# One group of scores per head pair from the third batch on, in an attention kernel followed by a feed-forward layer

## The chip, the cores and the metric

The kernel runs on one core of one Trainium2 chip. The time is device microseconds of one execution; what counts is the median of several. The engines are named as in the profile: PE (TensorE, matmuls), PEld (its weight loads), ACT (ScalarE), DVE (VectorE), POOL (GpSimd), SP (SyncE, which here only issues DMAs).

## The reference

Attention with a forget gate for 8 batches and 8 heads, 576 tokens, head width 64, and then a feed-forward layer over all 4608 tokens with 512 model columns and 2048 hidden ones:

```python
scores = scale * np.matmul(q, k.transpose(0, 1, 3, 2))
cum = np.cumsum(np.log(np.clip(f, 0.0001, 1.0)), axis=-1)
scores = np.where(causal, -1000000000.0, scores + cum[:, :, :, None] - cum[:, :, None, :])
attn = np.exp(scores - max) ; attn = attn / (sum + 1e-09)
x = np.matmul(attn, v)            # then heads side by side: 4608 x 512
h = x @ w_in
out = (h * (1.0 / (1.0 + np.exp(-h)))) @ w_out
```

## The kernel before

The decay factors are taken into the values: exp(-cum) of each key is multiplied into v, with one column of it kept as the 65th, so that a matmul of exponentials and values gives the outputs and the sums that they are divided by.

The first 128 queries of all heads are done in a prologue. The rest, 448 queries a head, is done in a loop over m = 0 to 15 (line 874, called a turn here), with two head pairs n = 2m and n + 1 in each; a batch has four head pairs, so m = 4 begins the third batch. For each head pair:

- `scores(n, c)`, lines 444 to 484: the scores, transposed, come in three chunks c = 0, 1, 2, each into one tile `sc` of two PSUM banks, one bank for each of the two heads. The two heads lie in partitions 0 to 63 and 64 to 127, so their matmuls (line 459) use half of the array's rows each. Then exponentials on ACT: 1024 wide for chunks 0 and 1 (line 463), 256 and 640 wide for chunk 2 (lines 463, 475). DVE masks with triangles (lines 468, 482).
- `attend(n)`, line 490: 28 matmuls of the exponentials with the values into one bank `dn` (lines 506, 515), then reciprocal and product on DVE into `xr` (lines 523, 524).
- `prepare(n)`, line 839: issues loads, casts on POOL and transposes by DMA for head pairs ahead. `back(m)`, line 531: turns the outputs of a turn, for m = 4 to 14 by DMA on SP, otherwise on PE.

The feed-forward layer is cut into pieces that are put between the attention's groups. An M1 piece (`m1_chunk`, line 560) is four matmuls into one bank `hp` (line 567), a tanh on ACT (line 575) and one product on DVE that reads both (line 576), after which the bank is free. An M2 piece (`m2_part`, line 594) is four matmuls 512 wide (line 612); four pieces fill one bank `po`, and the last of the four is followed by a copy `osb` on ACT (line 622), stored later from POOL's queue.

Which piece comes next is a planner's choice. `wanted` (line 641) keeps the M1 pieces of one group of tokens and the M2 pieces of the group before in step; `fill(us, least, ends)` (line 698) counts pieces at a fixed price (4 x (width / 2.4 + 2.5) ns) until `us` is used up, carries over what it went too far, and with `ends[0]` puts an M2 piece first. `slot(us, *ends)` calls it. `behind()` is the price of all pieces that are ready and not yet placed, and the last slot of a turn is the longer the more there is.

All engines work in the order in which the program states their instructions. PSUM's eight banks are two pools: `psc`, two buffers of two banks (tag "sc"), and `pbig`, four buffers of one bank (tag "big") for `hp`, `po`, `dn` and `tx`.

The loop's body before, whose lines matter for the change:

```python
scores(n, 0); scores(n, 1); prepare(n); back(m - 1); slot(2.4, 1, 0)
scores(n, 2); scores(n + 1, 0); prepare(n + 1);      slot(2.4, 1, 0)
scores(n + 1, 1); scores(n + 1, 2);                  slot(2.4, 1, 0)
attend(n); attend(n + 1);                            slot(0.8 to 3.5)
```

Of the kernel before, what the change touches and what calls it, by code (L numbers as in the profile page):

```python
# [8 lines left out]
ACT = mybir.ActivationFunctionType  # L9
ALU = mybir.AluOpType  # L10
FP32 = mybir.dt.float32
BF16 = mybir.dt.bfloat16
P = 128
# [5 lines left out]
def kernel(  # L19
# [10 lines left out]
    nc = tc.nc  # L30
# [410 lines left out]
    AT |= {(c, 0): SM + (c - 1) * P for c in range(1, NM)}  # L441
    AT |= {(2, 1): RB, (3, 1): SM + RB, (3, 2): 2 * SM}

    def scores(n, c):
        b, p = divmod(n, NP)
        if c == 0:
            us[n] = upool.tile([P, 2, UW], BF16, name="u", tag="u")
        u, ut = us[n], uts[n % 4]
        t = qkT[n]
        sc = psc.tile([P, 2, SM], FP32, name="sc", tag="sc")  # L450
        for kb, q0, q1, o in CHUNKS[c]:
            for i in range(2):
                r = slice(i * D, (i + 1) * D)
                if kb == 0:
                    kt = kT0[b][r, p, :]
                else:
                    k0 = RB if kb == NM else kb * P + RB
                    kt = t[r, k0 : k0 + P]
                nc.tensor.matmul(  # L459
                    sc[:, i, o : o + q1 - q0], lhsT=kt, rhs=t[r, q0:q1], start=True, stop=True  # L460
                )
        w = SM if c < 2 else T0
        nc.scalar.activation(  # L463
            out=u[:, :, c * SM : c * SM + w], in_=sc[:, :, 0:w], func=ACT.Exp, scale=scale
        )
        if c == 0:
            x = u[:, :, 0:RB].rearrange("p i (a t) -> p i a t", t=P)
            nc.vector.tensor_tensor(  # L468
                out=x,
                in0=x,  # L470
                in1=tri[:, None, None, :].to_broadcast([P, 2, NR, P]),
                op=ALU.mult,
            )
        if c == 2:
            nc.scalar.activation(  # L475
                out=ut[:, :, 0:3:2, :].rearrange("p k i t -> p i k t"),
                in_=sc[:, :, T0 : T0 + (NM + 1) * ST].rearrange("p i (k t) -> p i k t", t=ST),
                func=ACT.Exp,
                scale=scale,
            )  # L480
            x = ut[:, NM, 0:3:2, :]
            nc.vector.tensor_tensor(  # L482
                out=x, in0=x, in1=trit[:, None, :].to_broadcast([P, 2, ST]), op=ALU.mult
            )

    NGR = 2 * NR + 1

    BY_DMA = [2 * 2 <= m < NQ - 1 for m in range(NQ)]

    def attend(n):  # L490
        b, p = divmod(n, NP)
        if p % 2 == 0:
            xqs[n // 2] = xqp.tile([P, NGR, 2, D], BF16, name="xr", tag="xr", bufs=3)
        xq = xqs[n // 2]
        u, ut = us.pop(n), uts[n % 4]
        dn = pbig.tile([P, NGR, D + 1], FP32, name="dn", tag="big")

        def vals(kb, i):
            h = head(p, i)
            return v0[b][:, h, :] if kb == 0 else vbf[b][:, kb - 1, h, :]  # L500

        for i in range(2):
            for c in range(1, NM):
                for kb in range(c + 1):
                    o = AT[c, kb]
                    nc.tensor.matmul(  # L506
                        dn[:, i * NR + c - 1, :],
                        lhsT=u[:, i, o : o + P],
                        rhs=vals(kb, i),
                        start=(kb == 0),  # L510
                        stop=(kb == c),
                    )
        for i in range(2):
            for kb in range(NM + 1):
                nc.tensor.matmul(  # L515
                    dn[:, NGR - 1, :],
                    lhsT=ut[:, kb, i : i + 2, :].rearrange("p i t -> p (i t)"),
                    rhs=vals(kb, i),
                    start=(i == 0 and kb == 0),
                    stop=(i == 1 and kb == NM),  # L520
                )
        rec = recp.tile([P, NGR], FP32, name="rec", tag="rec")
        nc.vector.reciprocal(out=rec[:, :], in_=dn[:, :, D])
        nc.vector.tensor_tensor(  # L524
            out=xq[:, :, p % 2, :],
            in0=dn[:, :, 0:D],
            in1=rec[:, :, None].to_broadcast([P, NGR, D]),
            op=ALU.mult,
        )
# [58 lines left out]
    def store(n):  # L588
        n = max(n, 0)
        for q_, dst, src in stores[:n]:  # L590
            q_.dma_start(out=dst, in_=src)  # L591
        del stores[:n]
# [39 lines left out]
        nt = GW[g] // P  # L632
        M2 += [(g, tb, part) for tb in range(nt) for part in range(4)]
    M2_OF = [sum(1 for x in M2 if x[0] == g) for g in range(NG)]
    at = {"m1": 0, "m2": 0, "left": 0.0}
    ready: set[int] = set()
    open2 = {"w": False}

# [17 lines left out]
    def step(force=0):  # L656

        a, c = at["m1"], at["m2"]
        want = wanted(a, c)
        if not want:  # L660
            return None
        g1 = M1[a][0] if a < len(M1) else NG
        g2 = M2[c][0] if c < len(M2) else NG
        can1 = g1 in ready and not (M1[a][1] == 0 and g1 > g2 + 1)
        can2 = open2["w"] and c < len(M2) and g2 < g1
        kind = force if (force == 1 and can1) or (force == 2 and can2) else want
        if kind == 1:
            if M1[a][1] == 0:
                begin[g1] = (0, c)
            m1_chunk(g1, M1[a][1])  # L670
            at["m1"] += 1
            t = 4 * (GW[g1] / 2.4 + 2.5)
        else:
            m2_part(*M2[c])
            at["m2"] += 1
            t = 4 * (DM / 2.4 + 2.5)
        return t

    def behind():
        t = sum(4 * (GW[g] / 2.4 + 2.5) for g, _ in M1[at["m1"] :] if g in ready)  # L680
        t += sum(4 * (DM / 2.4 + 2.5) for g, _, _ in M2[at["m2"] :] if g in ready)
        return t / 1000
# [15 lines left out]
    def fill(us_, least=0, ends=(0, 0)):  # L698

        left = us_ + at["left"]  # L700
        kinds = plan(left)
        kinds += [0] * (least - len(kinds))
        if any(ends) and kinds:
            if 2 not in kinds:
                kinds[0] = 2
            n1, n2 = len(kinds) - kinds.count(2), kinds.count(2)
            e0 = 1 if ends[0] else 0
            e1 = 1 if ends[1] and n2 > e0 else 0
            inner = n2 - e0 - e1
            n = n1 + inner  # L710
            mid = [2 if (x + 1) * inner // n > x * inner // n else 1 for x in range(n)]
            if inner and mid[-1] == 2 and e1 and not e0:
                mid = mid[::-1]
            kinds = [2] * e0 + mid + [2] * e1
        for k in kinds:
            t = step(k)
            if t is None:
                at["left"] = 0.0
                return
            left -= t / 1000  # L720
        at["left"] = left
# [117 lines left out]
    def prepare(n):  # L839

        b, p = divmod(n, NP)
        if n > NP - 1 and n + 4 < NU:
            load_qk(n + 4)
        if 0 < n < NU - 2:
            cast_qk(n + 2)
            transposes(n + 2)
        if n < NP - 1:
            load_qk(n + 4)
        if b + 1 == B:
            return  # L850
        if p == 0 and b > 0:
            load_tails(b + 1)
        if b == 0 and p >= 2 or b > 0 and p == 1:
            for c in range(NM) if b > 0 else range(2 * (p - 2), 2 * (p - 1)):
                load_v(b + 1, c)
        if n == NP - 1:
            load_qk(n + 4)
        if p >= 2:
            for c in range(2 * (p - 2), 2 * (p - 1)) if b > 0 else range(NM * (p - 2)):
                convert_v(b + 1, c)  # L860
# [4 lines left out]
    def slot(us_, *ends):  # L865
        n = len(stores)
        fill(us_, 0, ends)
        store(n)
        for x in pending:
            x[0] -= 1  # L870
        while pending and pending[0][0] == 0:
            ready.update(pending.pop(0)[1])

    for m in range(NQ):
        n = 2 * m
        piece = 1.7 if m < 2 else 2.4
        scores(n, 0)
        scores(n, 1)
        prepare(n)
        if m > 0:  # L880
            back(m - 1)
            if m % 2 == 0:
                b = m // 2 - 1
                pending.append([2, [REST_OF[b]] + ([TAILS_OF[b][0]] if b == NM - 1 else [])])
        slot(piece, 1, 0)
        scores(n, 2)
        scores(n + 1, 0)
        prepare(n + 1)
        slot(piece, 1, 0)
        scores(n + 1, 1)  # L890
        scores(n + 1, 2)
        slot(piece, 1, 0)
        attend(n)
        attend(n + 1)
        slot(min(3.5, max(0.8, behind() - LAG)) if m > 1 else 0.8)
    back(NQ - 1)
    ready.update([REST_OF[B - 1], TAILS_OF[B - 1][0]])
    for x in pending:
# [35 lines left out]
```

The softmax here doesn't subtract the row's maximum and nothing guards it: scores larger than these inputs give would overflow.

## Time and profile before

| what | us |
|---|---|
| median of 13 runs | 344.75 (343.75 to 349.58) |
| the profiled execution's own time | 344.57 |
| its span, first to last instruction | 342.8 |
| PE busy | 335.8 |
| ACT busy | 216.7 |
| DVE busy | 182.0 |
| turns m = 4 to 15 | 108.0 to 279.9 of the span |
| feed-forward pieces alone, after the loop | 279.9 to 342.8 of the span |

A row of the profile's groups has the line, the engine, the operation, what it writes and reads with its shape, the count, the busy time in us, the mean of one in ns, and behind the second bar the idle time of the engine just before it with what ended it. The matmul ends are modelled: a 512-wide one lasts 0.38 us in the rows, though one starts every 0.216 us, so PE's holes are read from starts.

### The profile page before, as it was taken

The page shows a single profiled execution, that of the slowest core. Times are in us where ns is not written, and L with a number is a line of the kernel's source. Part 1 is how long each engine was busy: PE and PEld are TensorE (multiplying, and loading weights), DVE is VectorE, ACT ScalarE, POOL GpSimd, SP SyncE. Part 2 cuts the span into 40 slices and gives each one's busy share as a digit, 9 for nine tenths or more (in the row PEclk, how much of TensorE's full clock was granted, in tenths as well). Part 3 has the DMA queues.
Part 4 walks back from the last instruction along what each step waited for, and adds up shares of the span by engine and source line. Part 5 has one row for each costly group of instructions (what it writes and reads, how often), then busy time and mean ns, then how long its engine had stood idle before and what let it go on. Part 6 is the DMA issues. An engine that isn't in the chain of part 4 may idle for free.

```text
span 342.8 us, 8894 instructions
## 1 busy us (share of the span) xinstructions
PE 335.8 (98%) x3567; PEld 199.2 (58%) x3567; DVE 182.0 (53%) x389; ACT 216.7 (63%) x401; POOL 128.5 (37%) x227
## 2 busy tenths in 40 slices
PE   8999999999999999999999999999999999999995
PEld 3745656567656556566465666656656565555654
DVE  4766736467567367356446654556656464444330
ACT  5767645877687666857759677595685944454431
POOL 8895317724637154065037129208220000000011
PEclk9999999999999999999999999999999999999998
DMA  8999999999899996897796799789632010001012
GB/s 153 193 189 221 193 180 170 245 205 197 192 171 207 184 202 155 166 207 177 159 206 155 167 174 215 164 172 215 133 86 59 22 42 33 31 32 63 31 57 67
DMA packets 141497, 50.44 MB, mean 147 GB/s; under 512 B 132368, under 2 KB 138768, under 8 KB 141456
## 3 DMA queue, kind: packets, MB, share of 16 engines
q1 hardware_dynamic: 131440, 32.70, 52.2%
q0 software_dynamic: 9856, 17.04, 21.2%
q8 instruction: 28, 0.46, 0.6%
q10 hardware_dynamic: 160, 0.13, 0.1%
q14 instruction: 13, 0.11, 0.1%
HBM read 36.85 MB, written 9.44 MB: 135 GB/s over the span
## 4 chain that ended last, share of the span: by engine, by line
PE 68%; DMA 15%; POOL 7%; SPq 6%; issue 3%; ACT 0%; DVE 0%; POOLq 0%
PE po L612 29%; PE hp L567 25%; DMA vf<-in_v_dram 5%; PE sc L459 5%; PE dn L506 4%; DMA qktf<-in_k_dram 4%; DMA w_out_bf<-in_moe_w_out_dram 3%; SPq L427 3%; DMA qkT<-qkb 2%; SPq L158 2%; PE dn L515 2%; POOL vp L413 2%; PE wm L232 1%; POOL qkb L399 1%; SPq L168 1%
## 5 line engine op out<-in xcount | busy, mean ns | idle before, releaser
L576 DVE SCALAR_TENSOR_TENSOR gt<-th,hp 128x384 bf16<-128x384 bf16 (+2 forms) x208 | 105.6, 522 | 82.2 <-ACT th L575 78.9
L575 ACT ACTIVATE th<-hp 128x384 bf16<-128x384 f32 (+2 forms) x208 | 95.2, 479 | 84.4 <-PE hp L567 82.2
L612 PE MATMUL po<-w_out_bf,gt 128*128 128x512 bf16 (+1 forms) x592 | 145.3, 374 | 0.0
L567 PE MATMUL hp<-x,w_in_bf 128*128 128x384 bf16 (+2 forms) x704 | 128.2, 321 | 0.4 <-DVE xt L554 0.2
L567 PEld LDWEIGHTS <-w_in_bf 128*128 128x128 bf16 x832 | 79.9, 98 | 56.7 <-issue 0.5
L463 ACT ACTIVATE u<-sc 128x1024 bf16<-128x1024 f32 (+1 forms) x96 | 75.2, 822 | 10.2 <-PE sc L459 10.2
L612 PEld LDWEIGHTS <-gt 128*128 128x128 bf16 x592 | 53.3, 98 | 47.9 <-issue 2.5
L591 POOL DMA_DIRECT2D out_dram<-osb x38 | 21.0, 553 | 146.6 <-ACT osb L622 104.4
L413 POOL TENSOR_TENSOR vp<-vf,w_bf 128x520 bf16<-128x520 f32 (+1 forms) x32 | 34.0, 1067 | 24.7 <-DMA vf<-in_v_dram 19.8
L622 ACT ACTIVATE osb<-po 128x512 f32<-128x512 f32 (+1 forms) x37 | 22.1, 597 | 18.9 <-PE po L612 18.9
L468 DVE TENSOR_TENSOR u<-u,tri 128x768 bf16<-128x768 bf16 x32 | 22.1, 692 | 20.2 <-ACT u L463 20.2
L459 PE MATMUL sc<-qkT 64*128 64x128 bf16 (+1 forms) x640 | 26.7, 207 | 0.9 <-DMA qkT<-qkb 0.8
L399 POOL CAST qkb<-qf 128x384 bf16<-128x384 f32 x32 | 17.5, 548 | 24.0 <-PE tp L285 11.9
L482 DVE TENSOR_TENSOR ut<-ut,trit 128x128 bf16<-128x128 bf16 x32 | 9.3, 291 | 32.4 <-ACT ut L475 32.4
L459 PEld LDWEIGHTS <-qkT 64*128 64x128 bf16 x640 | 18.3, 94 | 12.3 <-issue 9.5
L475 ACT ACTIVATE ut<-sc 128x640 bf16<-128x640 f32 x32 | 23.3, 728 | 0.0
L506 PEld LDWEIGHTS <-u 128*128 128x128 bf16 x576 | 20.8, 97 | 2.5
L506 PE MATMUL dn<-vp,u 128*128 128x65 bf16 x384 | 21.8, 193 | 0.0
L524 DVE TENSOR_TENSOR xr<-dn,rec 128x448 bf16<-128x448 f32 x32 | 20.0, 624 | 1.1
L506 PE MATMUL dn<-v,u 128*128 128x65 bf16 x192 | 19.8, 193 | 0.0
L399 POOL CAST qkb<-kf 128x384 bf16<-128x384 f32 x32 | 17.3, 540 | 3.6 <-DMA kf<-in_k_dram 3.5
L567 PE MATMUL hp<-xt,w_in_bf 128*128 128x256 bf16 x128 | 17.7, 273 | 0.0
(68 smaller groups left out, 204.9 us busy)
## 6 DMA issues: line engine op xcount, KB each, us to landing
out_dram<-osb POOLq DMA_DIRECT2D x32, 256.0 KB, 3.3
vf<-in_v_dram SPq DMA_DIRECT2D x26, 256.0 KB, 4.9
qf<-in_q_dram SPq DMA_DIRECT2D x64, 96.0 KB, 3.4
kf<-in_k_dram SPq DMA_DIRECT2D x64, 96.0 KB, 3.0
w_in_bf<-in_moe_w_in_dram POOLq DMA_DIRECT2D x4, 512.0 KB, 7.0
w_out_bf<-in_moe_w_out_dram POOLq DMA_DIRECT2D x4, 512.0 KB, 9.6
vf<-in_v_dram POOLq DMA_DIRECT2D x6, 256.0 KB, 10.1
qkb<-in_q_dram POOLq DMA_DIRECT2D x8, 128.0 KB, 5.3
```

What stands on the lines that cost most here:

```text
L399: nc.gpsimd.tensor_copy(out=t2[:, c0 : c0 + NR, :].rearrange("p c x -> p (c x)"), in_=t[:, :, :, :].rearrange("p c h d -> p (c h d)"),)
L413: nc.gpsimd.tensor_tensor(out=vbf[b][r, c, :, :], in0=vst[b][c][r, :, :], in1=w_bf[r, c + 1, b * H : (b + 1) * H, None].to_broadcast([n, H ...
L459: nc.tensor.matmul(sc[:, i, o : o + q1 - q0], lhsT=kt, rhs=t[r, q0:q1], start=True, stop=True)
L463: nc.scalar.activation(out=u[:, :, c * SM : c * SM + w], in_=sc[:, :, 0:w], func=ACT.Exp, scale=scale)
L468: nc.vector.tensor_tensor(out=x, in0=x, in1=tri[:, None, None, :].to_broadcast([P, 2, NR, P]), op=ALU.mult,)
L475: nc.scalar.activation(out=ut[:, :, 0:3:2, :].rearrange("p k i t -> p i k t"), in_=sc[:, :, T0 : T0 + (NM + 1) * ST].rearrange("p i (k t) ...
L506: nc.tensor.matmul(dn[:, i * NR + c - 1, :], lhsT=u[:, i, o : o + P], rhs=vals(kb, i), start=(kb == 0), stop=(kb == c),)
L567: nc.tensor.matmul(hp[:, :], lhsT=w_in_bf[:, cc, fc * P : (fc + 1) * P], rhs=xcols(g, cc), start=(cc == 0), stop=(cc == NCC - 1),)
L575: nc.scalar.activation(out=th[:, :], in_=hp[:, :], func=ACT.Tanh, scale=0.5)
L576: nc.vector.scalar_tensor_tensor(out=gt[:, fc, :], in0=th[:, :], scalar=1.0, in1=hp[:, :], op0=ALU.add, op1=ALU.mult,)
L612: nc.tensor.matmul(po[:, :], lhsT=gt[:, fc, tb * P : (tb + 1) * P], rhs=w_out_bf[:, fc, m0:m1], start=(fc == 0), stop=(fc == NFC - 1),)
L622: nc.scalar.activation(out=osb[:, :], in_=po[:, :], func=ACT.Copy, scale=0.5)
```

## The change

From m = 4 on (`ONE_BY_ONE = 4`) the body of a turn is another:

- `all_scores(n)` does all three chunks of a head pair in one group: chunk 1 first, into two single banks of `pbig`, with one exponential 512 wide for each, then chunk 0 and chunk 2 into the two buffers of `psc`. The exponentials of chunk 2 are put on a list, `late`, and issued by `rest()` after the first M1 piece of the next slot, or after its second piece.
- The slots are 3.4, 3.4, 0.7 and at most 3.0 us; the second `attend` comes a slot after the first. The slot ahead of each group ends with an M2 piece and the slot behind it begins with one, where the planner has any; `fill` changes M1 into M2 pieces until there are two.
- `attend` writes to a buffer of `psc` in place of a bank of `pbig`.

For m below 4 the same work is done as before, apart from the M2 piece asked for at the end of the last slot of m = 3.

```diff
+    late: list = []
+    def exponentials(n, c, sc):
+        u, ut = us[n], uts[n % 4]
         w = SM if c < 2 else T0
+        if isinstance(sc, list):
+            for i in range(2):
+                nc.scalar.activation(
+                    out=u[:, i, c * SM : c * SM + w], in_=sc[i][:, :], func=ACT.Exp, scale=scale
+                )
+            return
...
+    def all_scores(n):
+        us[n] = upool.tile([P, 2, UW], BF16, name="u", tag="u")
+        sb = [pbig.tile([P, SM], FP32, name="sb", tag="big") for _ in range(2)]
+        products(n, 1, sb)
+        exponentials(n, 1, sb)
+        for c in (0, 2):
+            sc = psc.tile([P, 2, SM], FP32, name="sc", tag="sc")
+            products(n, c, [sc[:, i, :] for i in range(2)])
+            if c == 0:
+                exponentials(n, c, sc)
+            else:
+                late.append(lambda: exponentials(n, 2, sc))
...
+    ONE_BY_ONE = 4
...
-        dn = pbig.tile([P, NGR, D + 1], FP32, name="dn", tag="big")
+        if n // 2 < ONE_BY_ONE:
+            dn = pbig.tile([P, NGR, D + 1], FP32, name="dn", tag="big")
+        else:
+            dn = psc.tile([P, 2, SM], FP32, name="dns", tag="sc")
+            dn = dn[:, 0, 0 : NGR * (D + 1)].rearrange("p (c d) -> p c d", d=D + 1)
...
+        at["n"] += 1
+        if kind == 1 or at["n"] == 2:
+            rest()
         return t
+    def rest():
+        while late:
+            late.pop(0)()
...
-            if 2 not in kinds:
-                kinds[0] = 2
+            while kinds.count(2) < min(sum(ends), len(kinds)):
+                kinds[[k == 2 for k in kinds].index(False)] = 2
...
+        at["n"] = 0
         for k in kinds:
...
     def slot(us_, *ends):
         n = len(stores)
         fill(us_, 0, ends)
+        rest()
...
+        merged = m >= ONE_BY_ONE
+        piece = 3.4 if merged else 1.7 if m < 2 else 2.4
+        if merged:
+            all_scores(n)
+        else:
+            scores(n, 0)
+            scores(n, 1)
         prepare(n)
...
+        if merged:
+            slot(piece, 1, 1)
+            all_scores(n + 1)
+            prepare(n + 1)
+            slot(piece, 1, 0)
+            attend(n)
+            slot(0.7)
+            attend(n + 1)
+            slot(min(3.0, max(0.6, behind() - LAG)), 0, 1)
+            continue
...
-        slot(min(3.5, max(0.8, behind() - LAG)) if m > 1 else 0.8)
+        slot(min(3.5, max(0.8, behind() - LAG)) if m > 1 else 0.8, 0, int(m + 1 >= ONE_BY_ONE))
```

`products(n, c, banks)` is the old loop of score matmuls, with the bank of each head given to it.

More of the change, by code (lines that the diff above doesn't have):

```diff
@@ L442, with products @@
     AT |= {(2, 1): RB, (3, 1): SM + RB, (3, 2): 2 * SM}
-    def scores(n, c):
+    late: list = []
+    def products(n, c, banks):
         b, p = divmod(n, NP)
-        if c == 0:
-            us[n] = upool.tile([P, 2, UW], BF16, name="u", tag="u")
-        u, ut = us[n], uts[n % 4]
         t = qkT[n]
-        sc = psc.tile([P, 2, SM], FP32, name="sc", tag="sc")
         for kb, q0, q1, o in CHUNKS[c]:
@@ L459, in scores @@
                 nc.tensor.matmul(
-                    sc[:, i, o : o + q1 - q0], lhsT=kt, rhs=t[r, q0:q1], start=True, stop=True
+                    banks[i][:, o : o + q1 - q0], lhsT=kt, rhs=t[r, q0:q1], start=True, stop=True
                 )
+    def exponentials(n, c, sc):
+        u, ut = us[n], uts[n % 4]
         w = SM if c < 2 else T0
+        if isinstance(sc, list):
[4 more added lines that the diff above has]
+            return
         nc.scalar.activation(
@@ L484, in scores @@
             )
+    def scores(n, c):
+        if c == 0:
[4 more added lines that the diff above has]
+    def all_scores(n):
+        us[n] = upool.tile([P, 2, UW], BF16, name="u", tag="u")
+        sb = [pbig.tile([P, SM], FP32, name="sb", tag="big") for _ in range(2)]
+        products(n, 1, sb)
+        exponentials(n, 1, sb)
+        for c in (0, 2):
+            sc = psc.tile([P, 2, SM], FP32, name="sc", tag="sc")
+            products(n, c, [sc[:, i, :] for i in range(2)])
+            if c == 0:
+                exponentials(n, c, sc)
+            else:
+                late.append(lambda: exponentials(n, 2, sc))
     NGR = 2 * NR + 1
+    ONE_BY_ONE = 4
     BY_DMA = [2 * 2 <= m < NQ - 1 for m in range(NQ)]
@@ L634 @@
     M2_OF = [sum(1 for x in M2 if x[0] == g) for g in range(NG)]
-    at = {"m1": 0, "m2": 0, "left": 0.0}
+    at = {"m1": 0, "m2": 0, "left": 0.0, "n": 0}
     ready: set[int] = set()
@@ L875 @@
         n = 2 * m
-        piece = 1.7 if m < 2 else 2.4
-        scores(n, 0)
-        scores(n, 1)
+        merged = m >= ONE_BY_ONE
[5 more added lines that the diff above has]
+            scores(n, 1)
         prepare(n)
```

## The prediction

> **What bounds the kernel now.** I read the page first: busy rows and the clock line.
>
> ```profile
> PE 335.8 (98%) x3567; PEld 199.2 (58%) x3567; DVE 182.0 (53%) x389; ACT 216.7 (63%) x401; POOL 128.5 (37%) x227
> PEclk9999999999999999999999999999999999999998
> ```
>
> PE is busy 98% at full clock. A busy PE is not yet a packed PE, so I went on to who waits for whom:
>
> ```profile
> PEld L459 <- issue: 15.1, 47, 0.4
> PE sc L459 <- DMA qkT<-qkb: 0.8, 1, 0.8
> ```
>
> PE waits for ACT or DVE nowhere in the pair loop. The only regular hole is at the scores: of 48 groups of score matmuls (16 turns of m, three each), 47 show the weight load idle with nothing to wait for. PE's timeline at one group shows its cost:
>
> ```profile
> 150.06 0.81 PE L567 MATMUL hp<-x,w_in_bf 128*128 128x384 bf16 x4
> 150.81 0.40 PE L459 MATMUL sc<-qkT 64*128 64x128 bf16 x8
> 151.04 0.33 PE L459 MATMUL sc<-qkT,kT 64*128 64x384 bf16 x2
> 151.21 0.22 PE L459 MATMUL sc<-qkT 64*128 64x128 bf16 x2
> 151.35 0.39 PE L612 MATMUL po<-w_out_bf,gt 128*128 128x512 bf16 x1
> ```
>
> First column: start. Four 384-wide matmuls, one lasting 0.326, in 0.81 us start every 0.162, so the scores could start at 150.06 + 4 x 0.162 = 150.71; they start at 150.81, 0.10 late. The last score pair starts at 151.21 and needs 0.05 (eight 128-wide start at 150.81, the next pair at 151.04: 0.056 a pair); M2 starts at 151.35, 0.09 late. **A score group costs 0.19 us of holes**, however much is in it. Entry and exit of the outputs (L506, L515) show no such hole.
>
> Then the forms on ACT and DVE, mean ns at the end of "busy":
>
> ```profile
> L463 ACT ACTIVATE u<-sc 128x1024 bf16<-128x1024 f32 x64 | 64.5, 1035 | 10.2 <-PE sc L459 10.2
> L575 ACT ACTIVATE th<-hp 128x384 bf16<-128x384 f32 x128 | 61.9, 503 | 56.6 <-PE hp L567 55.3
> L475 ACT ACTIVATE ut<-sc 128x640 bf16<-128x640 f32 x32 | 23.3, 728 | 0.0
> L622 ACT ACTIVATE osb<-po 128x512 f32<-128x512 f32 x35 | 21.3, 609 | 16.3 <-PE po L612 16.3
> L463 ACT ACTIVATE u<-sc 128x256 bf16<-128x256 f32 x32 | 12.7, 395 | 0.0
> L575 ACT ACTIVATE th<-hp 128x512 bf16<-128x512 f32 x16 | 9.6, 597 | 5.9 <-PE hp L567 5.9
> L576 DVE SCALAR_TENSOR_TENSOR gt<-th,hp 128x384 bf16<-128x384 bf16 x128 | 69.1, 553 | 52.3 <-ACT th L575 49.4
> ```
>
> and how they queue, in a slot that begins with the last part of an M2 tile:
>
> ```profile
> 165.85 1.94 ACT L463 ACTIVATE u<-sc 128x1024 bf16<-128x1024 f32 x2
> 165.91 1.04 PE L612 MATMUL po<-w_out_bf,gt 128*128 128x512 bf16 x4
> 166.78 1.46 PE L567 MATMUL hp<-x,w_in_bf 128*128 128x384 bf16 x8
> 167.66 0.62 ACT L622 ACTIVATE osb<-po 128x512 f32<-128x512 f32 x1
> 168.13 0.53 ACT L575 ACTIVATE th<-hp 128x384 bf16<-128x384 f32 x1
> ```
>
> ACT works in the order written: exponentials, the copy of M2's result, then the tanh of an M1 chunk whose matmuls ended near 167.6. Two 1024-wide take 1.94, so a follower adds 0.905: its row less 0.13 (osb to th: 0.47). Until tanh and then gt on DVE have read hp, its bank is taken. Before, this costs nothing: ACT gets about 2 us of exponentials per slot.
>
> **What the Trainium skill says.** "TensorE: Matmul & The Clock Gate", Back-to-back issue gap, gives N/2.4 + 2.5 ns for a lone stream: 162.5 ns for 384, as here. Its Part 3, The mechanism, says that a weight load overlaps running matmuls only where the row group differs; scores load 64-row tiles into an array that a 128-row matmul fills, and the trace agrees that both switches cost about 0.1. "ScalarE: Activation LUTs", What ACT_TABLE_LOAD costs, prices an ACTIVATE at 186 ns + 0.833 per element, 613 for 512; the row shows 597, which I use. It lets followers overlap by 93 ns; the trace has 0.13, and that decides.
>
> **The change, part by part.** Times against the profiled execution's 344.57 (span 342.8); the median is 344.75, 0.05% above.
>
> 1. One group per head pair instead of three per two, from m = 4: 12 turns, 36 groups become 24. **-12 x 0.19 = -2.27 us**, directly on PE's path. The columns are unchanged; the split of the outputs adds no hole, by the above.
>
> 2. Middle chunk in two single banks: one 1024-wide ACTIVATE becomes two of 512: 0.48 + 0.48 for 0.905, +0.05 a head pair, 24 x 0.05 = 1.3 us of ACT, hidden while ACT idles (63% busy); not hidden, it is in the walk below.
>
> 3. The wait that this adds: the two "big" banks must be free when a group starts. "big" has four; the open po holds one. So at most **one** M1 chunk may be unread. Queued behind the waiting score matmul is all of PE. Walk for the first slot of a turn, PE ready at 0. PE: hole to 0.10, chunk 1 to 0.32, chunk 0 to 0.54, chunk 2 to 0.74 (0.056 per 128-wide pair and 0.162 per 384 as above, 0.029 per 64-wide pair from the same view), hole to 0.83, M2 (4 x 0.216 = 0.86) to 1.70, M1 chunks (0.65) to 2.35, 3.00, 3.65, M2 to 4.52; next group 4.62. ACT: chunk 1's matmuls end at 0.48; +0.035 (PE end to ACT, shortest regular gap between hp and th): exponentials start 0.51, 0.99; chunk 0 at 1.47; follower at 2.38. If the leading M2 piece ends a tile, osb 2.38 and the first tanh 2.85; then, by rest(), both of chunk 2 (3.24, 3.50), and the second tanh 4.09 to 4.58; its gt (0.553, 0.03 behind tanh's end in the timeline) 4.61 to 5.16; bank free 5.20. The group at 4.62 needs that bank: **stall 0.58**. Without osb all is 0.48 less with tanh waiting for its matmuls at 2.55: bank free at 4.90, stall 0.28. With two M1 chunks only the first has to be read: free at 3.97 with osb, group at 3.97: 0.
>
> Which slots are which follows from the planner's rule; stepping it through gives the old trace's order exactly, so I trust it for the new constants. M2-end M1 M1 M1 M2 in turns 5, 6, 7, 9, 14: 5 x 0.58 = 2.9. Turn 10, third M1 256 wide (0.437), group 0.21 earlier: 0.8. Turns 12 and 15, no osb: 2 x 0.28 = 0.56. Turn 4 (M1 first, two M2 last): 0.1. Turn 8 (two M1): 0. Turn 11: four 256-wide M1, the fourth waits for the first's bank, 3.54 - 3.01 = 0.53. Turn 13: second slot opens with M1 and has five in a row: 0.12 + 0.42. **Sum 5.4 us.** Unseen in the trace, the stall is bounded from 0 (no wait; it cannot be below) to a bank one gt later (+0.47 each).
>
> 4. Late chunk 2 and M2 on both sides: both are inside the walk. At the first group of a turn the last slot has left ACT idle (its M1 chunks come every 0.65, ACT needs 0.38), and an M1 two back was read 1.32 after its end while the group comes 1.61 after: 0.
>
> 5. Outputs in score banks: attend(n) waits for chunk 0's exponential, done 2.5 after its group's start; it comes at 3.8 or later. attend(n+1) waits for chunk 2's, 4.0 (4.5 with osb), and comes at about 5.3. The next turn's chunks wait for rec and xr (0.2 + 0.62), under the last slot of up to 3 us. Cost 0; without that cover about 0.5 a turn.
>
> 6. prepare(n+1) moves behind a longer slot: its casts (POOL), loads and transposes (SP) keep their order against back(m-1) and the stores in both queues, and have a full turn of 14 us before use, as before. Cost 0. Slots sum to 10.5 instead of 10.7 us; what is left goes to the tail, where PE is as packed.
>
> Sum: 344.57 - 2.27 + 5.4 = **347.7**, +0.9%.
>
> **Rivals.** (a) Faster: the banks come free in time, because M2 ahead of the group covers the readers. Against: 4.58 for the second tanh is plain addition of rows. For: margins are tenths, and all twelve hang on one guess about order. 344.57 - 2.27 = 342.3. It decides at 2.27/12 = 0.19 us of stall a turn: below is faster. (b) The two cancel: 344.6. (c) The group binds to a bank one gt later, or tanh of the second slot backs up as well: nine turns x 0.47 more, 347.7 + 4.2 = 351.9. (d) The M2 pieces asked for do not exist (turn 4 has none to start with): then M1 stands before a group, 1.3 from its release, like (c) in a few turns.
>
> **How the numbers follow.** Main case 0.55, own range 345.8 to 350.5; (a) 0.22; (b) 0.10; (c) and (d) 0.13. About 0.3% (1 us) is what a measurement can tell here. Faster 0.22, same 0.13, slower 0.65. (a) must be inside, (c) may be left out: 342.0 to 350.5.
>
> **What would show it.** 24 score groups after m = 4 with 0.32 "issue" each, 36 in all; new PE waits at the scores' line released by DVE gt, about 0.6 each in turns 5, 6, 7, 9, 14, nearly none in turn 8; ACT without idle from a turn's first group to its second. If PE shows no wait for DVE at the second group, step 3 is wrong and the time is near 342.3. If waits stand at dn instead, step 5 is.

## The result, and the profile after

| kernel | median us | lowest to highest | ratio to before, 95% interval |
|---|---|---|---|
| before (48 runs) | 345.12 | 343.31 to 349.58 | |
| changed (11 runs) | 354.52 | 349.02 to 356.40 | 1.0172 (1.0132 to 1.0212) |
| changed, again (`e1_unchanged`, 4 runs) | 355.11 | 354.60 to 355.57 | 1.0303 (1.0287 to 1.0319) |

The change makes the kernel slower, by more than was predicted: 347.7 was forecast with 342.0 to 350.5 around it. The executions lie in two clusters, two near 349 and eight near 354 to 356, with one at 351.63 between them; the first ratio leaves most of the upper cluster out as disturbed, the repeat shows that it is the usual case. Two profiles of the same kernel therefore stand here, one at 349.02 (span 347.2), one at 354.60 (span 352.8).

The busy line of the first one's page:

```profile
PE 336.0 (97%) x3567; PEld 202.3 (58%) x3567; DVE 182.7 (53%) x389; ACT 219.2 (63%) x425; POOL 127.5 (37%) x227
```

PE is busy as long as before (336.0 against 335.8 us), and the span is 4.4 us longer, so the busy time does not tell what happened. The waits of PE do (who waited, for whom; total us, times, longest), in the execution at 349.02:

```profile
PE sb L457 <- DVE gt L612: 2.6, 6, 0.7
PE hp L603 <- DVE gt L612: 1.6, 2, 1.1
...
PE po L648 <- DVE xt L590: 0.5, 1, 0.5
```

Before, PE waited for no DVE instruction at the scores. In the changed kernel six score groups (`sb`, the two general banks) and two M1 chunks wait for `gt`, the DVE product that frees an M1 bank. The same view of the execution at 354.60:

```profile
PE dns L551 <- DVE ut L490: 3.2, 1, 3.2
PE sb L457 <- DVE gt L612: 2.8, 6, 1.0
PE hp L603 <- DVE gt L612: 1.6, 2, 1.1
```

The bank waits are nearly the same. On top comes **one** wait of 3.2 us, at the outputs, for the mask of the last 64 queries.

**The bank wait**, in the timeline of turn 5 of the execution at 349.02 (start, length, both in us; in brackets the idle time before):

```profile
121.84 0.34 PE L457 MATMUL sb<-qkT,kT 64*128 64x384 bf16 x2
122.26 1.09 ACT L467 ACTIVATE u<-sb 128x512 bf16<-128x512 f32 x2 [0.69 <-PE sb L457]
123.23 1.03 ACT L471 ACTIVATE u<-sc 128x1024 bf16<-128x1024 f32 x1
124.14 0.62 ACT L658 ACTIVATE osb<-po 128x512 f32<-128x512 f32 x1
124.61 0.53 ACT L611 ACTIVATE th<-hp 128x384 bf16<-128x384 f32 x1
124.98 0.43 ACT L471 ACTIVATE u<-sc 128x256 bf16<-128x256 f32 x1
125.25 0.77 ACT L483 ACTIVATE ut<-sc 128x640 bf16<-128x640 f32 x1
125.83 0.95 ACT L611 ACTIVATE th<-hp 128x384 bf16<-128x384 f32 x2
126.04 0.84 DVE L490 TENSOR_TENSOR ut<-ut,trit 128x128 bf16<-128x128 bf16 x1 [0.32 <-ACT ut L483]
126.37 0.33 PE L457 MATMUL sb<-qkT,kT 64*128 64x384 bf16 x1
126.81 1.01 DVE L612 SCALAR_TENSOR_TENSOR gt<-th,hp 128x384 bf16<-128x384 bf16 x2
127.41 0.32 PE L457 MATMUL sb<-qkT,kT 64*128 64x384 bf16 x1 [0.70 <-DVE gt L612]
```

The order on ACT is the one walked through in the prediction. PE starts the first head's matmul of the second group at 126.37 and the second head's at 127.41, when the first of the two `gt` has ended (126.81 + 0.55): the second bank was not free. Of the 1.04 between the two starts 0.16 would pass anyway; 0.87 is the wait. The mask at 126.04 stands on DVE ahead of that `gt`, and at 0.84 us it is longer than the 0.23 us that it usually takes; this comes back below.

**The mask wait**, in turn 12 of the execution at 354.60. First GpSimd (POOL) alone:

```profile
233.14 1.08 POOL L627 DMA_DIRECT2D out_dram<-osb  x2 [7.68 <-ACT osb L658]
234.21 0.52 POOL L399 CAST qkb<-qf 128x384 bf16<-128x384 f32 x1
234.66 0.51 POOL L399 CAST qkb<-kf 128x384 bf16<-128x384 f32 x1
235.11 0.29 POOL L403 CAST qkb<-qktf 128x128 bf16<-128x128 f32 x1
235.37 2.06 POOL L413 TENSOR_TENSOR vp<-vf,w_bf 128x520 bf16<-128x520 f32 x2
237.38 0.49 POOL L399 CAST qkb<-qf 128x384 bf16<-128x384 f32 x1
237.83 0.50 POOL L399 CAST qkb<-kf 128x384 bf16<-128x384 f32 x1
238.28 0.28 POOL L403 CAST qkb<-qktf 128x128 bf16<-128x128 f32 x1
238.53 2.17 POOL L413 TENSOR_TENSOR vp<-vf,w_bf 128x520 bf16<-128x520 f32 x2
```

DVE and PE at the same time:

```profile
234.13 5.53 DVE L490 TENSOR_TENSOR ut<-ut,trit 128x128 bf16<-128x128 bf16 x1 [0.32 <-ACT ut L483]
239.59 1.01 DVE L612 SCALAR_TENSOR_TENSOR gt<-th,hp 128x384 bf16<-128x384 bf16 x2
239.72 0.20 PE L551 MATMUL dns<-vp,ut 128*128 128x65 bf16 x1 [3.19 <-DVE ut L490]
```

This mask usually lasts 0.226 us (the median of its 32). Here its row says 5.53, and GpSimd works without a gap from 234.21 to 239.58: nine instructions, casts and value products for two head pairs. The mask ends 0.08 us after the ninth of them, and the tenth starts only then. DVE counts as busy all that time: here a wait stands in the profile as a long instruction, not as idle time. In the execution at 349.02 the same row of GpSimd broke off after one product, because the next values had not landed:

```profile
234.41 1.05 POOL L413 TENSOR_TENSOR vp<-vf,w_bf 128x520 bf16<-128x520 f32 x1
236.13 1.05 POOL L413 TENSOR_TENSOR vp<-vf,w_bf 128x520 bf16<-128x520 f32 x1 [0.68 <-DMA vf<-in_v_dram]
```

and there the mask took 2.38 us, from 233.17 to 235.55, and ended in the gap that begins at 235.45. Between these two executions the difference is thus whether a load of values had landed when GpSimd came to it. The windows after the long wait (us, busy us and counts by engine, granted clock, DMA):

```profile
239.70:243.20 3.50, 3.33 (x17) 1.74 (x19) 3.43 (x9) 0.98 (x2) 1.00 (x1) 0.72 0.00 0
243.20:246.70 3.50, 3.50 (x35) 1.61 (x34) 0.88 (x2) 1.78 (x4) 0.00 (x0) 0.79 0.34 66
```

After 3.2 us of idleness PE's granted clock is 0.72 and 0.79 for two stretches of 3.5 us: 3.5 x 0.28 + 3.5 x 0.21 = 1.7 us more. (It is one spell of 3.41 us at 0.50, from 241.25 on.) The 5.6 us between the two spans can be placed from PE's starts: in turn 12 PE loses 3.6 us at 354.60 and 0.66 at 349.02, a difference of 3.0; the clock makes 1.7; turn 5's bank wait is 1.15 where it was 0.87, another 0.3; and 0.7 is lost before turn 4, ahead of all that was changed. The clock of the other executions fits: all but one of those on record near 354 to 356 show a mean of 0.990 to 0.995, the three below 352 show 0.998 or more.

### The profile page after: what moved, and what is told of

It is laid out like the page before. It is cut to its first block, busy times and chain, and to the rows that moved or that the text cites. A ratio compares the mean times of both kernels' runs of the same rounds, so it can differ in the third digit from the quotient of the medians.

```text
span 347.2 us, 8917 instructions
## 1 busy us (share of the span) xinstructions
PE 336.0 (97%) x3567; PEld 202.3 (58%) x3567; DVE 182.7 (53%) x389; ACT 219.2 (63%) x425; POOL 127.5 (37%) x227
## 4 chain that ended last, share of the span: by engine, by line
PE 78%; ACT 9%; DVE 4%; issue 3%; DMA 3%; POOL 1%; POOLq 0%
PE po L648 33%; PE hp L603 29%; PE sc L457 4%; PE dns L542 3%; ACT u L471 3%; ACT u L467 2%; PE sb L457 2%; DVE gt L612 2%; ACT th L611 2%; PE dns L551 2%; DMA vf<-in_v_dram 2%; PE tp L285 1%; DMA qkb<-in_k_dram 1%; PE dn L542 1%; ACT ut L483 1%
## 5 line engine op out<-in xcount | busy, mean ns | idle before, releaser
L603 PE MATMUL hp<-x,w_in_bf 128*128 128x384 bf16 (+2 forms) x704 | 126.9, 321 | 0.8 <-DVE gt L612 0.5
L648 PEld LDWEIGHTS <-gt 128*128 128x128 bf16 x592 | 54.3, 98 | 47.5 <-DVE xt L590 0.9
L471 ACT ACTIVATE u<-sc 128x1024 bf16<-128x1024 f32 (+1 forms) x72 | 53.6, 763 | 2.5 <-PE sc L457 2.5
L476 DVE TENSOR_TENSOR u<-u,tri 128x768 bf16<-128x768 bf16 x32 | 21.0, 655 | 55.3 <-ACT u L471 55.3
L467 ACT ACTIVATE u<-sb 128x512 bf16<-128x512 f32 x48 | 26.2, 602 | 14.7 <-PE sb L457 14.7
L457 PEld LDWEIGHTS <-qkT 64*128 64x128 bf16 x640 | 19.9, 94 | 8.2 <-issue 6.9
L457 PE MATMUL sc<-qkT 64*128 64x128 bf16 (+1 forms) x592 | 22.2, 205 | 0.1
L490 DVE TENSOR_TENSOR ut<-ut,trit 128x128 bf16<-128x128 bf16 x32 | 11.7, 366 | 14.7 <-ACT ut L483 14.7
L542 PE MATMUL dns<-vp,u 128*128 128x65 bf16 x288 | 16.3, 193 | 0.0
L560 DVE TENSOR_TENSOR xr<-dns,rec 128x448 bf16<-128x448 f32 x24 | 15.0, 624 | 0.8
```

The lines of the kernel that those rows point to most:

```text
L457: nc.tensor.matmul(banks[i][:, o : o + q1 - q0], lhsT=kt, rhs=t[r, q0:q1], start=True, stop=True)
L467: nc.scalar.activation(out=u[:, i, c * SM : c * SM + w], in_=sc[i][:, :], func=ACT.Exp, scale=scale)
L471: nc.scalar.activation(out=u[:, :, c * SM : c * SM + w], in_=sc[:, :, 0:w], func=ACT.Exp, scale=scale)
L542: nc.tensor.matmul(dn[:, i * NR + c - 1, :], lhsT=u[:, i, o : o + P], rhs=vals(kb, i), start=(kb == 0), stop=(kb == c),)
L603: nc.tensor.matmul(hp[:, :], lhsT=w_in_bf[:, cc, fc * P : (fc + 1) * P], rhs=xcols(g, cc), start=(cc == 0), stop=(cc == NCC - 1),)
L648: nc.tensor.matmul(po[:, :], lhsT=gt[:, fc, tb * P : (tb + 1) * P], rhs=w_out_bf[:, fc, m0:m1], start=(fc == 0), stop=(fc == NFC - 1),)
```

## The experiments

**Unchanged.**

> The changed kernel once more, nothing edited. Its profiled execution took 349.0 and its median is 354.5, so about 5.5 us of the median are in no profile yet. Bank theory (the second score group of a turn waits until DVE has read an M1 bank, behind chunk 2's exponentials on ACT): the same waits in every execution, 349 to 350. Rival (a wait that comes in some executions only, a DMA that lands late or a lower granted clock): times in two clusters, near 349 and near 354 to 355, and a profile of the upper cluster has one more PE wait of several us at one place, or a clock below 0.998.

Measured: 355.11 (354.60 to 355.57), all four in the upper cluster, with the profile read above. What the rival expected is there: one more wait, and the clock at 0.995. The bank waits alone do not make the time.

**Chunk 2's exponentials one M1 piece later.**

```diff
-        if kind == 1 or at["n"] == 2:
+        at["k"] = at["k"] + (kind == 1)
+        if at["k"] == 2 or (at["k"] == 0 and at["n"] == 2):
             rest()
```

> Chunk 2's exponentials are issued after the second M1 piece of the slot, not after the first. Bank theory: the second tanh no longer stands behind them, its bank is read by about 4.5 us after the slot's start and the group comes at 4.6, so the waits at the second group of turns 5, 6, 7, 9, 10, 12, 14, 15 (3.9 us in the profile of the changed kernel) go: 345 to 346 where the changed kernel has 349. Rival (the group as such, or the execution-dependent part, makes the time): no gain over 1 us, and two clusters as before.

Measured: 344.47 (343.73 to 347.29), ratio 0.9993 (0.9969 to 1.0016), profile at 344.41, a little below the 345 to 346 that were expected. Its PE waits inside the loop:

```profile
PE hp L603 <- DVE gt L612: 1.0, 2, 0.7
...
PE hp L603 <- DVE xt L590: 0.5, 1, 0.5
PE po L648 <- DVE xt L590: 0.5, 1, 0.5
```

(Rows named "issue" at `po` are left out: this trace lacks 43 of the 592 M2 matmuls.) No score group waits for a `gt` any more, and the mask's longest is 0.82. In turn 12 the mask took 0.75 beside three casts, and behind these casts GpSimd then stood idle for 2.86 us, so the long row did not come about. This experiment takes away the whole 10 us, but it cannot share them out between the two causes; the next two do. Its weight-load view also shows the saving of the change by itself, 35 holes where before had 47:

```profile
PEld L457 <- issue: 12.3, 35, 0.4
```

**Without the mask in turn 12.**

```diff
+            if n // 2 == 12:
+                return
             x = ut[:, NM, 0:3:2, :]
             nc.vector.tensor_tensor(
```

> The changed kernel without the triangle mask on the last 64 queries (DVE, trit) for the two head pairs of turn 12; that masking is left out of the result. In the profile at 354.6 this one instruction lasted 5.53 us where it usually lasts 0.23, beside an unbroken row of GpSimd casts and products, and the outputs waited 3.35 us for it, after which PE ran at half clock for about 3.4 us. Port theory (the mask and GpSimd wait for each other): all executions near 349, a gain of 5 to 6 us on the median, the score-bank waits of the other turns unchanged. Rival (GpSimd's row only happens to lie there; DVE is late for another reason): the next DVE instruction of turn 12 is as late, and the median stays near 354.

Measured: 349.29 (348.75 to 349.88), all in the lower cluster. Two DVE instructions left out of 389 give 5.2 us. GpSimd's row is still there, the same nine instructions without a gap from 233.72 to 239.08, and beside it the other DVE instructions of turn 12 keep their usual length:

```profile
233.72 0.52 POOL L399 CAST qkb<-qf 128x384 bf16<-128x384 f32 x1
...
238.04 2.17 POOL L413 TENSOR_TENSOR vp<-vf,w_bf 128x520 bf16<-128x520 f32 x2
...
234.02 1.02 DVE L614 SCALAR_TENSOR_TENSOR gt<-th,hp 128x384 bf16<-128x384 bf16 x2 [0.70 <-ACT th L613]
235.19 0.62 DVE L562 TENSOR_TENSOR xr<-dns,rec 128x448 bf16<-128x448 f32 x1
235.73 1.01 DVE L614 SCALAR_TENSOR_TENSOR gt<-th,hp 128x384 bf16<-128x384 bf16 x2
```

So the rival falls, and this profile is not one in which the row happened to break off. The pause of 0.08 us after the ninth instruction is here too, without the mask, so the mask did not make it.

**The output stores of turns 11 and 12 from SP's queue**, with nothing left out.

```diff
-                q_ = nc.gpsimd if not last else (nc.scalar if n == 1 else nc.sync)
+                q_ = (nc.sync if at["now"] in (11, 12) else nc.gpsimd) if not last else (nc.scalar if n == 1 else nc.sync)
```

> The changed kernel with the output stores of turns 11 and 12 issued from SP's queue instead of GpSimd's; nothing is left out. In both profiles of the changed kernel GpSimd stood 7.68 us behind two such stores, waiting for the copy osb, and then ran what had piled up in one row, into which the tail mask of turn 12 fell. Port theory: without these stores the casts and products run earlier and with gaps, the mask of turn 12 lasts under 1 us, and the executions lie near 349, as without the mask. Rival (the row of GpSimd work has another cause, its loads): the row and the long mask stay, 354 to 355.

Measured: 349.45 (348.39 to 349.63), ratio 1.0107 (1.0067 to 1.0148). GpSimd's timeline beside turns 11 and 12:

```profile
220.74 0.51 POOL L399 CAST qkb<-qf 128x384 bf16<-128x384 f32 x1 [2.54 <-DMA qf<-in_q_dram]
221.46 0.51 POOL L399 CAST qkb<-kf 128x384 bf16<-128x384 f32 x1 [0.20 <-DMA kf<-in_k_dram]
224.92 0.30 POOL L403 CAST qkb<-qktf 128x128 bf16<-128x128 f32 x1 [2.96 <-DMA qktf<-in_k_dram]
233.27 2.23 POOL L413 TENSOR_TENSOR vp<-vf,w_bf 128x520 bf16<-128x520 f32 x2 [8.05 <-DMA vf<-in_v_dram]
```

The casts that stood in the row at 234 run at 221 to 225, with gaps. The mask of turn 12 starts at 234.18, just before the first product ends at 234.32, and takes 0.23; a pause of 0.12 follows that product. So the wait behind a store, which keeps GpSimd's next casts back until they come in one row, is what put the mask in trouble, and it is enough to take away either the mask or the row. The lower cluster, 1.1% above before, is the net cost of the bank waits, less the holes saved; some of these waits are themselves lengthened by masks in other turns, as shown below.

**A shorter first slot.**

```diff
-            slot(piece, 1, 1)
+            slot(2.6, 1, 1)
...
-            slot(min(3.0, max(0.6, behind() - LAG)), 0, 1)
+            slot(min(3.8, max(0.6, behind() - LAG)), 0, 1)
```

> The first slot of a turn is 2.6 instead of 3.4 us and the last at most 3.8 instead of 3.0: one or two M1 chunks stand between the two groups, not three; the order of the exponentials is left as it is. Bank theory: waits at the second group only in turns 6 and 8, where M1 M1 without an M2 piece stands ahead of it (0.9 us each by the plain walk), none in the others: 344.5 to 346. Rival (ACT's burst as such holds PE up): the waits move to other places and the time stays within 1 us of the changed kernel.

Measured: 348.18 (346.99 to 348.57), ratio 1.0091 (1.0068 to 1.0113). A miss: 344.5 to 346 was expected. The mask's longest is 1.13 and no output waits for it, so the mask does not explain this. PE's waits for ACT and DVE in the loop:

```profile
PE sc L457 <- ACT ut L483: 1.0, 2, 0.6
PE hp L603 <- DVE gt L612: 0.9, 2, 0.7
PE po L648 <- DVE gt L612: 0.9, 2, 0.5
...
PE sb L457 <- DVE gt L612: 0.5, 1, 0.5
```

The wait at `sb` shrank from 2.6 to 0.5, but with less PE work between the two groups the second one meets chunk 2's score bank before its exponential is done (`sc` for ACT), and the M2 tile opened behind the group finds no bank (`po` for `gt`). The rival, that ACT's burst holds PE up wherever it next needs a bank, is right here, if the time is held against the lower cluster, which lies about 1 us higher: a shorter cover moves the wait.

**The outputs back in a general bank**, on top of e2 (`if True:` in place of `if n // 2 < ONE_BY_ONE:`).

> Chunk 2's exponentials after two M1 pieces, as in e2, and the outputs back in a general bank in all turns. Bank theory: at attend a general bank must be free beside the open M2 tile and one or two unread M1 banks; by the walk it is free within 0.3 us in most turns: 0.5 to 1.5 us above e2, 345 to 346. Rival (the outputs in score banks were what made the merged turn work): waits of about 1 us at the outputs in most of the twelve turns, 352 or more.

Measured: 346.09 (344.91 to 350.30, 20 runs), 1.6 above e2, just past the expected range; ratio 1.0029 (1.0012 to 1.0047). By the ratios to before the step from e2 is 1.2 us, and the two intervals overlap a little, so about 1 us is what the outputs in score banks are worth. They did not hurt.

**No M2 piece ahead of a group**, on top of e2 (ends 1, 0 for the first slot, none for the last).

> As e2, with no M2 piece asked for ahead of a score group (only behind it). In turns 5, 7, 9 and 12 four M1 chunks then run straight into the second group. Bank theory: each of these waits for two banks, about 0.6 us, and little elsewhere: 2 to 3 us above e2, 346.5 to 347.5. Rival (ACT drains fast enough, so the M2 piece ahead does nothing): within 0.5 us of e2.

Measured: 347.58 (346.49 to 348.77), 3.1 above e2, or 2.4 by the ratios; ratio 1.0062 (1.0033 to 1.0091). Waits of 0.4 to 0.9 us follow the second group in turns 5, 7 and 9, and one of 1.0 stands at it in turn 12: the turns are those that were named, the sizes are not all 0.6. Another 0.8 us comes from turn 11, whose wait is 1.30 where e2 had 0.47. The rival falls.

**Other slot sizes**, on top of e2: 3.4, 2.6, 1.3 and at most 3.4 us, run twice.

> As e2, with slots of 3.4, 2.6, 1.3 and at most 3.4 us in place of 3.4, 3.4, 0.7 and 3.0: the planner's order then has fewer runs of four or more M1 chunks and fewer groups without an M2 piece ahead. Bank theory: of the some 2.3 us of bank waits that e2 still has, half go: 343 to 344. Rival (the sizes don't matter once chunk 2's exponentials are late): 344.5.

> The kernel of e7 once more (chunk 2's exponentials after two M1 pieces; slots of 3.4, 2.6, 1.3 and at most 3.4 us), to settle its sign against the kernel before. Bank and port theories: faster by 0.2 to 0.5%, most executions 343 to 344.5. Rival (e7's gain was the chip's scatter): the interval of the ratio holds 1.

Measured: 344.02 (343.08 to 352.18), ratio 0.9968 (0.9949 to 0.9988); again 343.52 (342.80 to 345.38), ratio 0.9960 (0.9939 to 0.9981). One of the 23 executions took 352.18, the others at most 345.38. This version is 0.3 to 0.4% faster than the kernel before. In its first profile no score group waits for DVE; the longest wait inside the loop is one of 0.6 us at an M1 bank.

## Why the prediction was wrong, step by step

- **Step 1, the holes: right.** -2.27 us were put on 12 groups fewer; entry and exit still cost 0.096 and 0.093 each. It also removed something not counted: in the profile of before, turn 4's middle group waited 1.0 us for its transposed q and k, which the later second group does not.
- **Step 2, two exponentials for one: right that it stays hidden outside the walk.** ACT is busy 219.2 instead of 216.7 us, 2.5 more where 1.3 was reckoned.
- **Step 3, the bank wait: the mechanism right, the sum short.** Read from the starts of the matmuls at 349.02 against the prediction: turns 6, 7, 9, 14 0.50 each (0.58), turn 10 0.71 (0.80), turns 12 and 15 0.16 (0.28), turn 8 none (none); but turn 5 0.87 (0.58), turn 4 0.64 (0.1, at the M2 tile's bank, not at the group), turn 11 1.30 (0.53), turn 13 0.80 (0.54), and 0.66 more within turn 12 behind the mask. Sum 7.3 instead of 5.4. With -2.27 and -1.0 this gives +4.0 us; the span says +4.4, and 0.4 is not placed. This part alone would have landed inside the range. About 1.9 of the 7.3 belong to the masks, see step 6. What is left meets the 5.4 partly by luck: turns 4 and 13 came out 0.8 above the walk, and the others together 0.8 below it.
- **Step 6, prepare and GpSimd at cost 0: the step that failed.** It asked only whether GpSimd's work would be ready in time, not what that work holds up while it runs; and the walk of step 3, which lets `gt` follow 0.03 behind its tanh, left the masks on DVE out altogether. `e4` and `e8` show that the last mask of turn 12 and an unbroken row of casts and products do not go together; that costs 3.2 us in one turn and 1.7 of clock afterwards, in most executions, and it is what separates 349 from 354.5. The trace of before had the sign: the same mask, median 0.226, lasts up to 0.929 there.

```profile
L482 DVE TENSOR_TENSOR ut<-ut,trit x32: 224/226/929, 65.0 to 274.3; 128x128 bf16<-128x128 bf16 x32
```

  The same thing made step 3 short. In turn 5 the mask of 128 columns stands ahead of the `gt` that PE waits for. It took 0.27, 0.65, 0.84 and 1.12 us in `e8`, `e4` and the executions at 349.02 and 354.60, and PE's wait at the second group was 0.50, 0.67, 0.87 and 1.15. In turn 11 the mask of 768 columns, median 0.559, took 1.38 beside two products of GpSimd:

```profile
211.29 1.38 DVE L476 TENSOR_TENSOR u<-u,tri 128x768 bf16<-128x768 bf16 x1 [2.38 <-ACT u L471]
```

  If turn 11's wait grew by as much as its mask, the masks make 0.37 + 0.82 + 0.66 = 1.9 us in turns 5, 11 and 12; this is an estimate from these rows.

  The Trainium skill has a reason ("SBUF — State Buffer", Who interferes with whom): a DVE instruction with two SBUF inputs contends with a GpSimd instruction that reads SBUF, because its second input comes through a read interface that the two engines share. The mask multiplies two SBUF tiles; `gt`, whose second input is in PSUM, kept its 0.55 us beside GpSimd's row in `e4`. The runs agree as far as they go; none measured the port itself.
- **Steps 4 and 5: right.** No wait stands at the first group of a turn, and none at the outputs for their bank. By `e6` and `e5` the M2 pieces ahead are worth 2 to 3 us and the score banks for the outputs about 1, so both help.
- **The rivals.** (a): the waits at the groups went only where the exponentials were moved, in `e2`, which is level with before, and `e7`, which is faster. (d) does not show: the first group of turn 4 has M1 pieces ahead of it and does not wait. None of the rivals was the mask.

What stays open: the split of turn 4's 0.64 us between its transposes and its M2 tile; and what decides the cluster in general. The landing of the values is read from two profiles, and no run varied that load. Nor is a long row always waited out: in `e3` the mask of turn 12 met the same three casts, took 1.13 us and ended after the second cast, where GpSimd shows no pause. The changed kernel was not run again beside `e4` and `e8`; that they would have met the long mask is read from `e4`'s row above and from the stores that hold GpSimd back in both profiles of the changed kernel.

## What to carry to other kernels

Where groups are merged to save switches, add up the reader's queue between two groups: a bank is free only when the last reader has passed everything written ahead of it, so place the long readers behind the short ones that free what PE needs next. Here one moved line gave 10 us, about half of it because the row of GpSimd work then broke. Look for instructions whose longest row is many times the median, and ask what they share with what runs beside them; a queue held back by an early store can run its backlog right into them. In the traced execution of the upper cluster, the long wait also cost the clock behind it.

## What was not expected of the hardware

- A 0.226 us DVE mask lasted 5.53 us beside nine GpSimd instructions back to back; in the two profiles of the changed kernel it got through where GpSimd paused for 0.08 (239.58 to 239.66) or 0.68 us. Beside the same row in `e4`, DVE instructions with one input in PSUM kept their 0.55 and 0.62 us.
- One idle stretch of 3.2 us on PE was followed, 1.5 us after PE had started again, by 3.4 us at half clock: a 384-wide matmul every 0.320 us in place of 0.162.
- Switching PE between 64-row and 128-row matmuls costs 0.09 to 0.10 us each way in these traces, whatever stands on the other side (M1, M2 or a transpose).
